# Seven quarter products in place of eight for the second matrix product of a fused attention and channel-mixer kernel

## The chip, the cores and the metric

The kernel runs on one core of a Trainium2 chip. The metric is the device time of one execution in microseconds (us). A core has a matrix engine (TensorE, PE in the profile, with its weight loads as PEld), two engines for elementwise work (VectorE, DVE; ScalarE, ACT), GpSimd (POOL), and queues that issue transfers (SP for most small ones, GpSimd for the large loads). Matrix products are written into PSUM banks of 128 partitions by 512 fp32 numbers; VectorE or ScalarE has to read a bank out before it can be used again.

## The reference

Selective attention over 8 batches, 8 heads, 576 positions, head size 64, then a low-rank sequence mixer and a channel mixer. What the change touches is the last line but one:

```
x = attention(q, k, v, s)            # per batch 576 x 512
h = (x^T @ U) @ V                    # rank 32, along the sequence
u = x + h^T                          # 576 x 512 per batch
ch = max(u @ w_ch1, 0) @ w_ch2       # 512 -> 2048 -> 512
return u + ch
```

`w_ch1` is 512 x 2048 and `w_ch2` 2048 x 512. The kernel takes and gives fp32 and multiplies in bf16.

## The kernel before

Heads are worked on in pairs: n = 0 to 31, four pairs to a batch. For each pair there are three generators, each of which yields after a piece of work:

- `transposes(n)` turns q and k with TensorE into two `pwork` banks; VectorE (for some n ScalarE) copies them into a `slot` (L309, L312). SP adds four bias rows to the slot from a table in HBM (L273).
- `scores(n)` multiplies q and k into `pscore` banks and a small `pwork` tail (L376), ScalarE takes the exponential into `pT` (L391, L402, L408), and VectorE masks (L321).
- `values(n)` multiplies pT with v into two `pwork` banks (L436); VectorE takes a reciprocal (L445) and scales into `x_sb` (L446).

`seqmix(b)` is the low-rank mixer of a batch: `up` (L465), a copy `uxT` on VectorE (L474), a product with the identity (L478), a copy `ux` on VectorE (L480), a product into one `pscore` pair and two `pwork` banks (L510), and their evacuation with an add on VectorE into `uT` (L490), with a small product for the last 64 rows (L535).

`chanmix(g)` is the channel mixer of 512 rows; there are nine groups (0 to 8), and group g needs rows of the batches g-1 and g. It has 16 steps of the first product: hidden tile nf is four matmuls of 128 x 512 into one `pwork` bank (L622), which ScalarE rectifies into `hT` as bf16 (L654). Then come four row tiles i of the second product, each 16 matmuls of 512 columns into one bank (L632); VectorE adds `u_sd`, a copy of uT turned back by a DMA transpose (L692), and SP writes the rows out (L709). The last row tile of group 8 is split into 384 and 128 columns (L669, L676, L682). Group 0 adds u by matmuls instead (L700, L708).

`pwork` has four banks that are given out in turn, `pscore` two double banks. Everything above that goes through `pwork`, the hidden tiles included, takes the next of its four.

The steps of `chanmix` are woven between the steps of attention as filling: `step_fill()` adds `pace[1]` to a counter after each attention step and lets one filling step run when the counter reaches 16. In the main loop (n = 8 to 33) the pace is 11 at first and 13 from the second batch on. What is left of the groups when attention ends runs alone with pace 16. In the steady part a batch takes about 38.5 us; from about 300 us on only groups remain.

The order of TensorE and of GpSimd is the order in which the program is written. For VectorE, ScalarE and SP that holds in the first part of the kernel; after that the scheduler of the tile framework puts their instructions into a fixed order when the kernel is built. All engines then execute their own order strictly one after another; each instruction waits on semaphores for what it needs.

Loads: GpSimd issues q, k and v of batch b+1 at the start of batch b (`load`, L111 and L182); v has three slots in rotation (`v_slots`), `slot` five, `uT` four, `u_sd` two.

Of the kernel before, what the change touches and what calls it, by code (L numbers as in the profile page):

```python
# [16 lines left out]
ALU = mybir.AluOpType  # L17
# [22 lines left out]
def kernel(  # L40
# [130 lines left out]
    def init_v(eng, vt):  # L171
        eng.memset(vt[64:, 4, :, :], 0.0)
        eng.memset(vt[:, 0:4, :, D : D + 1], 1.0)
        eng.memset(vt[0:64, 4, :, D : D + 1], 1.0)

    def load_v(b, parts=range(5)):
        vt = v_slots[b % 3]
        if b < 3:
            init_v(nc.gpsimd, vt)
        for t in parts:  # L180
            rows_t = 128 if t < 4 else 64
            nc.gpsimd.dma_start(  # L182
                out=vt[:rows_t, t, :, 0:D],
                in_=v[b, :, ds(t * 128, rows_t), :].rearrange("h p d -> p h d"),
            )
# [10 lines left out]

    SK = 5 * 128
    slots = [consts.tile([128, 2, S + SK], BF16, name=f"slot{i}") for i in range(NSLOT)]
    for slot in slots:
        nc.vector.memset(slot[:KA, :, 2 * S :], 0.0)  # L200

# [24 lines left out]
    for r, n_r, c in ((0, 3, 1), (3, 1, 0)):  # L226
# [4 lines left out]

    w1_sb = consts.tile([128, 4, FF], BF16)
    w2_sb = consts.tile([128, NF, DM], BF16)
    nc.gpsimd.dma_start(
        out=U_sb[:, :4, 0:R], in_=moe_U[:512].rearrange("(kt kp) r -> kp kt r", kp=128)
    )
# [18 lines left out]

    def uT(g):
        if g not in uT_of:
            uT_of[g] = work.tile([128, 4, 512], BF16, tag="uT", name="uT", bufs=4)
        return uT_of[g]


# [5 lines left out]

    def transposes(n):
        b, hp = divmod(n, PB)
        slot = slots[n % NSLOT]  # L270
        if b > 0:
            for r, n_r, c in ((0, 3, 1), (3, 1, 0)):
                nc.sync.dma_start(  # L273
                    out=slot[ds(D + r, n_r), :, ds(c * S, S)],
                    in_=rows_hbm[ds(r, n_r), ds(2 * n, 2)],
                )
        tps = {}

        def turn(hh, c):
            if c == 0:  # L280
                tile = pwork()
                if (n, hh) == (3, 0):
                    spin(2, tile)
                tps[hh] = tile.bitcast(BF16)[:, : 2 * 4 * TP].rearrange(
                    "p (c t m) -> p c t m", c=2, t=4
                )
            src = (q_t[b], k_t[b])[c]
            for t2 in range(4):
                nc.tensor.transpose(  # L289
                    tps[hh][:, c, t2, :],  # L290
                    src[:, 2 * hp + hh, ds(t2 * 128, 128)],
                    identity[:TP, :TP],
                )

        if b == 0:
            for hh in range(2):
                turn(hh, 0)
            yield
        for hh in range(2):
            if b > 0:  # L300
                turn(hh, 0)
            turn(hh, 1)
            tp = tps[hh]
            dst = slot[0:D, hh, 0 : 2 * S]
            for par in range(2):
                src = tp[par * D : par * D + D]
                if in_runs(b):
                    by_run = dst.rearrange("p (c t two m) -> p c t two m", c=2, t=4, two=2)
                    copies(n, hh, par)(by_run[:, :, :, par, :], src)  # L309
                else:  # L310
                    in_turn = dst.rearrange("p (c m t two) -> p c m t two", c=2, t=4, two=2)
                    copies(n, hh, par)(  # L312
                        in_turn[:, :, :, :, par], src.rearrange("p c t m -> p c m t")
                    )
            yield
# [54 lines left out]
        yield  # L370

    def scores(n, pT, spins=()):
        slot = slots[n % NSLOT]

        def mm(dst, hh, j, lo, hi):
            nc.tensor.matmul(  # L376
                dst,
                lhsT=slot[0:KA, hh, ds(S + j * 128, 128)],
                rhs=slot[0:KA, hh, lo:hi],
                start=True,  # L380
                stop=True,
            )

        tail = None
        for hh in range(2) if n > 0 else ():
            near = pscore()
            for j in range(4):
                mm(near[:, ds(j * 128, 128)], hh, j, j * 128, j * 128 + 128)
            mm(near[:, 512:960], hh, 0, 128, S)
            mm(near[:, 960:1024], hh, 3, 512, S)  # L390
            nc.scalar.activation(pT[:, hh, 0:1024], near, EXP, scale=scale)  # L391
            if n >= PB:
                mask(pT[:, hh, 0:512].rearrange("p (a b) -> p a b", a=4), 4, 128)
            if spins:
                tail = tail or pwork()
                spin(spins[hh], tail)
            yield
        mid, tail = pscore(), tail or pwork()
        for hh in range(2):
            mm(mid[:, ds(hh * 512, 320)], hh, 1, 256, S)  # L400
            mm(mid[:, ds(hh * 512 + 320, 192)], hh, 2, 384, S)
        nc.scalar.activation(  # L402
            pT[:, :, 1024:1536], mid.rearrange("p (a b) -> p a b", a=2), EXP, scale=scale
        )
        yield
        for hh in range(2):
            mm(tail[:, ds(hh * 64, 64)], hh, 4, 512, S)
        nc.scalar.activation(  # L408
            pT[:, :, 1536:1600],
            tail[:, 0:128].rearrange("p (a b) -> p a b", a=2),  # L410
            EXP,
            scale=scale,
        )
        if n >= PB:
            mask(pT[:, :, 1536:1600], 2, 64)
        yield
# [7 lines left out]
    def values(n, pT):  # L424
        b, hp = divmod(n, PB)
        if hp == 0:
            x_of[b] = work.tile([128, PB, 5, 128], BF16, tag="x_sb", name="x_sb")
            if b >= FT:
                xT_of[b] = work.tile([128, 4, 640], BF16, tag="xT", name="xT", bufs=1)
        x_sb, vt = x_of[b], v_slots[b % 3]  # L430
        for hh in range(2):
            h = 2 * hp + hh
            po = pwork()[:, : 5 * (D + 1)].rearrange("p (i d) -> p i d", i=5)
# [196 lines left out]
    def outputs(f2, hT, i, nfs, more=True):  # L630
        for nf in nfs:
# [8 lines left out]
            if nf % 4 == 3 and nf < nfs[-1]:  # L640
                yield

    def chanmix(g, hT=None, done=0):
        u = uT_of.pop(g)
        if g > 0:
            hT = work.tile([128, NF, 512], BF16, tag="hT", name="hT")
            u_sd = work.tile([128, 4, 4, 128], BF16, tag="u_sd", name="u_sd")
            nc.sync.dma_start_transpose(
                out=u_sd.rearrange("p a b c -> p (a b) c"), in_=u.rearrange("p a b -> p (a b)")
            )  # L650
        for nf in range(done, NF):
            f1 = pwork()
            hidden(f1, u, nf, range(4))
            nc.scalar.activation(hT[:, nf, :], f1, RELU)  # L654
            yield
        ahead = {}
        if g == 0:
            for i in range(2):
# [2 lines left out]
                    yield  # L661
                yield
        for i in range(4):
            if g == NG - 1 and i == 3:
                o_sb = work.tile([128, DM], FP32, tag="o_sb", name="o_sb", bufs=3)
                for lo, hi in ((0, 3), (3, 4)):
                    f2 = pwork()
                    for nf in range(NF):
                        nc.tensor.matmul(  # L669
                            f2[:, lo * 128 : hi * 128],  # L670
                            lhsT=hT[:, nf, ds(i * 128, 128)],
                            rhs=w2_sb[:, nf, lo * 128 : hi * 128],
                            start=(nf == 0),
                            stop=(nf == NF - 1),
                        )
                    nc.vector.tensor_tensor(  # L676
                        o_sb[:, lo * 128 : hi * 128].rearrange("p (a b) -> p a b", b=128),
                        f2[:, lo * 128 : hi * 128].rearrange("p (a b) -> p a b", b=128),
                        u_sd[:, lo:hi, i, :],
                        op=ALU.add,  # L680
                    )
                    nc.sync.dma_start(  # L682
                        out=out_flat[ds(g * 512 + i * 128, 128), lo * 128 : hi * 128],
                        in_=o_sb[:, lo * 128 : hi * 128],
                    )
                return
            f2 = ahead[i] if i in ahead else pwork()
            for _ in outputs(f2, hT, i, range(8 if i in ahead else 0, NF), g == 0):
                yield
            o_sb = work.tile([128, DM], FP32, tag="o_sb", name="o_sb", bufs=3)  # L690
            if g > 0:
                nc.vector.tensor_tensor(  # L692
                    o_sb.rearrange("p (a b) -> p a b", a=4),
                    f2.rearrange("p (a b) -> p a b", a=4),
                    u_sd[:, :, i, :],
                    op=ALU.add,
                )
            else:
                for dt in range(4):
                    nc.tensor.matmul(  # L700
                        f2[:, ds(dt * 128, 128)],
# [128 lines left out]
    def load(b):  # L830
        alloc_qk(b)
        for h in range(0, H, 4 if b == 2 else H):
            load_qk(b, h, 4 if b == 2 else H)
        load_v(b)

    load(2)
    fill.append(chanmix(0, first_hT, 4))
    pace[1] = 0
    made = {}
# [33 lines left out]
    for n in range(2 * PB, NP + 2):  # L873
# [20 lines left out]
            fill_with(1)  # L894
        if hp == 1 and b > FT:
            fill.append(chanmix(b - 1))
            pace[1] = 13
        if 2 * PB < n <= NP:
            run(values(n - 1, pT_of(n - 1)))
    pace[1] = 16  # L900
    fill.append(chanmix(NG - 1))
    while fill:
# [32 lines left out]
```

The softmax here doesn't subtract the row's maximum and nothing guards it: scores larger than these inputs give would overflow.

## Time and profile before

| | us |
|---|---|
| median of 9 executions | 375.37 |
| lowest and highest | 374.77, 381.16 |
| the profiled execution | 374.77 |
| its span, first to last instruction | 373.0 |
| TensorE busy | 364.5 |
| ScalarE busy | 199.1 |
| VectorE busy | 189.9 |
| GpSimd busy | 83.3 |

All parts of the profile come from this one execution. The span leaves out 1.8 us that lie around the first and last instruction. Matmuls are pipelined, so a matmul's own duration (379 ns for 512 columns) is longer than the distance to the next one; the latter is what counts for a row of them. TensorE is busy 9 tenths or more of nearly every fortieth of the span, and its clock is granted in full. In a row of instruction groups the columns are: line, engine, operation, output <- inputs, shapes, count, then busy time and mean duration of one, then idle time of the engine just before them and what ended it. Line numbers are those of the kernel before.

### The profile page before, as it was taken

How to read it: one execution, taken by the hardware profiler on the slowest of the kernel's cores; microseconds unless marked ns; L12 is line 12 of the kernel's file. 1: busy time of each engine (PE TensorE's matmuls, PEld its weight loads, DVE VectorE, ACT ScalarE, POOL GpSimd, SP SyncE). 2: the span in 40 equal slices, each digit the busy share in tenths (PEclk: the TensorE clock that was granted, in tenths of full speed). 3: DMA queues.
4: the chain of work that ended last, by engine and by line, in shares of the span. 5: the costliest groups of instructions: out<-in, count | busy, mean ns of one | idle time of the engine just before them, and what ended most of it. 6: DMA issues, size and time to landing. Idle time of an engine off the chain costs nothing.

```text
span 373.0 us, 8446 instructions
## 1 busy us (share of the span) xinstructions
PE 364.5 (98%) x3524; PEld 211.4 (57%) x3583; DVE 189.9 (51%) x446; ACT 199.1 (53%) x301; POOL 83.3 (22%) x108
## 2 busy tenths in 40 slices
PE   8999999999999999999999999999999999999996
PEld 4675566666655565556656565666565544444443
DVE  8876777585567545755475437653653142002011
ACT  3876965757742776067804782378435611621710
POOL 8997437115103600251006100000000000000000
PEclk9999999999999999999999999999999999999999
DMA  7999999999997993699969994210323043302002
GB/s 106 171 204 203 174 186 114 162 153 94 120 79 133 132 112 57 138 104 110 65 125 109 133 74 90 86 53 18 58 76 92 19 39 125 64 30 84 0 30 84
DMA packets 143534, 37.34 MB, mean 100 GB/s; under 512 B 130632, under 2 KB 137896, under 8 KB 143496
## 3 DMA queue, kind: packets, MB, share of 16 engines
q0 software_dynamic: 104640, 18.49, 84.9%
q1 hardware_dynamic: 38856, 18.31, 27.4%
q8 instruction: 28, 0.46, 0.6%
q14 instruction: 10, 0.08, 0.1%
HBM read 37.25 MB, written 9.70 MB: 126 GB/s over the span
## 4 chain that ended last, share of the span: by engine, by line
PE 92%; DVE 3%; ACT 2%; issue 2%; ACTq 0%
PE pwork L632 32%; PE pwork L622 31%; PE pscore L376 10%; PE pwork L436 7%; PE pwork L289 4%; PE pscore L338 1%; DVE slot L312 1%; PE pscore L205 1%; PE pwork L669 1%; PE pscore L622 1%; PE pwork L465 1%; DVE x_sb L446 1%; ACT pT L402 1%; PE pscore L510 1%; ACT pT L391 0%
## 5 line engine op out<-in xcount | busy, mean ns | idle before, releaser
L622 PE MATMUL pwork<-uT,w_sb 128*128 128x512 bf16 x533 | 134.0, 379 | 1.7 <-ACT pT L408 0.2
L632 PE MATMUL pwork<-w_sb,hT 128*128 128x512 bf16 x531 | 129.9, 379 | 1.8 <-DVE slot L312 0.2
L654 ACT ACTIVATE hT<-pwork 128x512 bf16<-128x512 f32 x140 | 84.8, 609 | 74.1 <-PE pwork L622 74.0
L391 ACT ACTIVATE pT<-pscore 128x1024 bf16<-128x1024 f32 x56 | 56.2, 1029 | 60.8 <-PE pscore L376 60.7
L622 PEld LDWEIGHTS <-w_sb 128*128 128x128 bf16 x576 | 50.8, 98 | 49.6 <-issue 0.6
L632 PEld LDWEIGHTS <-hT 128*128 128x128 bf16 x560 | 49.2, 98 | 49.0 <-issue 1.7
L321 DVE TENSOR_TENSOR pT<-pT,keep 128x512 bf16<-128x512 bf16 (+1 forms) x81 | 28.8, 355 | 59.8 <-ACT pT L391 36.0
L376 PE MATMUL pscore<-slot 68*128 68x320 bf16 (+1 forms) x500 | 54.6, 246 | 0.2
L376 PEld LDWEIGHTS <-slot 68*128 68x128 bf16 x564 | 41.6, 97 | 22.9 <-issue 1.3
L692 DVE TENSOR_TENSOR o_sb<-pwork,u_sd 128x512 f32<-128x512 f32 x31 | 21.4, 690 | 58.3 <-PE pwork L632 57.7
L436 PEld LDWEIGHTS <-pT 128*128 128x128 bf16 x870 | 33.1, 98 | 11.0 <-issue 0.3
L182 POOL DMA_DIRECT2D v_slot<-in_v_dram x36 | 30.3, 852 | 29.8 <-issue 17.7
L436 PE MATMUL pwork<-v_slot,pT 128*128 128x65 bf16 x870 | 35.3, 193 | 0.0
L309 DVE COPY slot<-pwork 64x576 bf16<-64x576 bf16 x70 | 31.7, 453 | 5.3 <-PE pwork L289 4.7
L446 DVE TENSOR_TENSOR x_sb<-pwork,rec 128x320 bf16<-128x320 f32 x64 | 31.5, 492 | 2.2
L402 ACT ACTIVATE pT<-pscore 128x1024 bf16<-128x1024 f32 x29 | 30.3, 1044 | 1.9 <-PE pscore L376 1.0
L312 DVE COPY slot<-pwork 64x576 bf16<-64x576 bf16 x35 | 28.1, 802 | 5.9 <-PE pwork L289 4.0
L111 POOL DMA_DIRECT2D q_sd<-in_q_dram x5 | 11.2, 2235 | 86.2 <-PE pwork L289 84.3
L445 DVE RECIPROCAL rec<-pwork 128x5 f32<-128x5 f32 x64 | 12.3, 192 | 24.4 <-PE pwork L436 24.0
L289 PEld LDWEIGHTS <-q_sd 72*128 72x128 bf16 x256 | 14.6, 98 | 9.7 <-DMA q_sd<-in_q_dram 0.9
L289 PE MATMUL pwork<-identity,q_sd 72*128 72x72 bf16 x256 | 18.4, 197 | 0.1
L289 PE MATMUL pwork<-identity,k_sd 72*128 72x72 bf16 x256 | 18.0, 197 | 0.0
(110 smaller groups left out, 223.3 us busy)
## 6 DMA issues: line engine op xcount, KB each, us to landing
out_dram<-o_sb SPq DMA_DIRECT2D x35, 256.0 KB
w_sb<-in_moe_w_ch_dram POOLq DMA_DIRECT2D x4, 1024.0 KB, 12.8
v_slot<-in_v_dram POOLq DMA_DIRECT2D x28, 128.0 KB, 16.2
q_sd<-in_q_dram POOLq DMA_DIRECT2D x5, 576.0 KB, 11.6
k_sd<-in_k_dram POOLq DMA_DIRECT2D x5, 576.0 KB, 17.8
q_sd<-in_q_dram POOLq DMA_DIRECT2D x4, 288.0 KB, 15.4
k_sd<-in_k_dram POOLq DMA_DIRECT2D x4, 288.0 KB, 14.1
q_sd<-in_q_dram POOLq DMA_DIRECT2D x4, 144.0 KB, 4.3
```

Source lines behind the costliest of these rows:

```text
L182: nc.gpsimd.dma_start(out=vt[:rows_t, t, :, 0:D], in_=v[b, :, ds(t * 128, rows_t), :].rearrange("h p d -> p h d"),)
L289: nc.tensor.transpose(tps[hh][:, c, t2, :], src[:, 2 * hp + hh, ds(t2 * 128, 128)], identity[:TP, :TP],)
L309: copies(n, hh, par)(by_run[:, :, :, par, :], src)
L312: copies(n, hh, par)(in_turn[:, :, :, :, par], src.rearrange("p c t m -> p c m t"))
L376: nc.tensor.matmul(dst, lhsT=slot[0:KA, hh, ds(S + j * 128, 128)], rhs=slot[0:KA, hh, lo:hi], start=True, stop=True,)
L391: nc.scalar.activation(pT[:, hh, 0:1024], near, EXP, scale=scale)
L402: nc.scalar.activation(pT[:, :, 1024:1536], mid.rearrange("p (a b) -> p a b", a=2), EXP, scale=scale)
L436: nc.tensor.matmul(po[:, i, :], lhsT=pT[:, hh, ds(place(j, i), 128)], rhs=vt[:, j, h, :], start=(j == 0), stop=(j == i), skip_group_check= ...
L446: nc.vector.tensor_tensor(x_sb[:, hp, :, ds(hh * D, D)], po[:, :, 0:D], rec.to_broadcast([128, 5, D]), op=ALU.mult,)
L622: nc.tensor.matmul(f1, lhsT=w1_sb[:, kt, ds(nf * 128, 128)], rhs=u[:, kt, :], start=(kt == 0), stop=(kt == 3),)
L632: nc.tensor.matmul(f2, lhsT=hT[:, nf, ds(i * 128, 128)], rhs=w2_sb[:, nf, :], start=(nf == 0), stop=(nf == NF - 1 and not more), skip_grou ...
L654: nc.scalar.activation(hT[:, nf, :], f1, RELU)
```

## The change

For groups 1 to 8 the second product is cut into quarters. With the hidden matrix A (512 rows by 2048) and w2 (2048 by 512),

```
A = [A11 A12]   rows 0-255        B = [B11 B12]   hidden 0-1023
    [A21 A22]   rows 256-511          [B21 B22]   hidden 1024-2047
```

the plain way has eight products of quarters. The change forms sums and makes seven, a form of Strassen's scheme:

```
A_1 = A21 + A22   A_2 = A_1 - A11   A_3 = A11 - A21   A_4 = A12 - A_2
B_1 = B12 - B11   B_2 = B22 - B_1   B_3 = B22 - B12   B_4 = B21 - B_2
p1 = A11 B11   p2 = A12 B21   p3 = A_4 B22   p4 = A22 B_4
p5 = A_1 B_1   p6 = A_2 B_2   p7 = A_3 B_3
C11 = p1 + p2             U2 = p1 + p6
C12 = U2 + p5 + p3        C21 = U2 + p7 + p4       C22 = U2 + p7 + p5
```

(The code subtracts B_4 the other way round from the classical scheme, so that all results are sums.) Each product is 2 x 8 matmuls of 256 columns into one `pwork` bank. The sums of w2 are formed once by GpSimd (12 instructions after the load of batch 2, and four at the start of group 1, which overwrite B12). The sums of A are formed by VectorE in halves of 128 x 1024 bf16; two of the eight are issued after hidden tiles 12 and 14, the others during p1, p2 and p6. A_1, A_2 and A_4 lie in two slots and one v slot that are no longer used otherwise; A_3 overwrites A21 in `hT`. The sums of the products with u are eleven VectorE instructions of 128 x 512 in fp32 and one copy of p1 on ScalarE. Outputs are written by quarters of 256 rows by 256 columns.

To make room, `slot` uses three of its five tiles from n = 8 on, v two of its three slots from batch 3 on (so `load_v` moves to the end of an iteration), `uT` has three buffers, `u_sd` one, and u_sd's transpose is issued at hidden tile 3. A group has 30 filling steps instead of 32, and the pace of the main loop becomes 12.

```diff
+    def weight_sums():
+        for dst, a, b in ((B_1, B12, B11), (B_2, B22, B_1), (B_4, B21, B_2)):
+            for k2 in range(0, HF, 2):
+                at = (slice(None), slice(k2, k2 + 2))
+                nc.gpsimd.tensor_sub(dst[at], a[at], b[at])
...
+    def total(dst, a, b, op, k4):
+        at = (slice(None), slice(4 * k4, 4 * k4 + 4))
+        nc.vector.tensor_tensor(dst[at], a[at], b[at], op=op)
+
+    def first_sums(hT, one):
+        if one:
+            total(A_1, hT[:, :HF, 256:], hT[:, HF:, 256:], ALU.add, 0)
+        else:
+            total(A_2, A_1, hT[:, :HF, :256], ALU.subtract, 0)
...
+        def product(acc, a, b, i):
+            for kt in range(HF):
+                nc.tensor.matmul(
+                    acc[:, i, :],
+                    lhsT=a[:, kt, ds(i * 128, 128)],
+                    rhs=b[:, kt, :],
+                    start=(i == 0 and kt == 0),
+                    stop=(kt == HF - 1),
+                    skip_group_check=True,
+                )
...
+        p1 = bank()
+        for i in halves:
+            product(p1, A11, B11, i)
+            total(*((A_1, A21, A22, ALU.add), (A_2, A_1, A11, ALU.subtract))[i], 1)
+            yield
+        nc.scalar.copy(U2, p1)
+        p2 = bank()
+        for i in halves:
+            product(p2, A12, B21, i)
+            total(A_3, A11, A21, ALU.subtract, i)
+            yield
+        o = quarter()
+        add_u(o, U2, 0, 0)
+        add(o, o, p2)
+        send(o, 0, 0)
+        p6 = bank()
+        for i in halves:
+            product(p6, A_2, B_2, i)
+            total(A_4, A12, A_2, ALU.subtract, i)
+            yield
+        add(U2, U2, p6)
+        p5 = bank()
...
+        add(o22, U2, p5)
+        p3 = bank()
...
+                add_u(o12, o22, 0, 1)
...
+        add(o12, o12, p3)
+        send(o12, 0, 1)
+        p7 = bank()
...
+                add_u(o22, o22, 1, 1)
...
+        add(U2, U2, p7)
+        add(o22, o22, p7)
+        send(o22, 1, 1)
+        p4 = bank()
...
+                add_u(o21, U2, 1, 0)
...
+        add(o21, o21, p4)
+        send(o21, 1, 0)
...
+            if g > 0 and nf in (12, 14):
+                first_sums(hT, nf == 12)
...
-        load_v(b)
 
     load(2)
+    load_v(2)
+    weight_sums()
...
-            pace[1] = 13
+            pace[1] = 12
...
+        if hp == 0 and 2 <= b < B - 1:
+            load_v(b + 1)
```

## The prediction

> **What bounds the kernel now.** I read the busy shares first, then the busy time by stretch, then the chain of waits, then the rows of the operations concerned, last the end of the timeline.
>
> The engines over the whole span:
>
> ```profile
> PE 364.5 (98%) x3524; PEld 211.4 (57%) x3583; DVE 189.9 (51%) x446; ACT 199.1 (53%) x301; POOL 83.3 (22%) x108
> ```
>
> TensorE (PE) is the only full engine. The same by stretch (columns: length, then busy time of PE, weight loads, VectorE, ScalarE, GpSimd; one batch of the steady part, the last stretch, in which the mixer runs alone):
>
> ```profile
> 148.64:187.09 38.45, 38.07 (x399) 22.64 (x407) 21.19 (x54) 22.16 (x35) 8.68 (x7) 1.00 1.67 107
> ...
> 330.00:373.00 43.00, 39.97 (x198) 18.97 (x200) 5.69 (x9) 9.55 (x16) 0.00 (x0) 1.00 0.14 50
> ```
>
> VectorE (DVE) has 17.3 us free in a batch of 38.45 us, and nearly everything in the last stretch. The chain of waits in order of time (start, length, what):
>
> ```profile
> 86.65 1.04 PE pwork L436 x30
> ...
> 342.51 9.28 PE pwork L622 x43
> ...
> 366.68 3.51 PE pwork L669 x32
> ```
>
> The chain is TensorE's own order. From it come the paces: 9.28/43 = 0.2158 us for a matmul of 512 columns; 16 of 384 with 16 of 128 take 3.51 us; the 30 of 65 columns, each with its own weight load, take at most 1.04 us, under 0.035 us each. So columns set the pace and weight loads hide, down to 65 columns. The rows I price VectorE and ScalarE with (busy, mean ns, idle before):
>
> ```profile
> L321 DVE TENSOR_TENSOR pT<-pT,keep 128x512 bf16<-128x512 bf16 x54 | 22.8, 422 | 36.2 <-ACT pT L391 36.0
> L692 DVE TENSOR_TENSOR o_sb<-pwork,u_sd 128x512 f32<-128x512 f32 x31 | 21.4, 690 | 58.3 <-PE pwork L632 57.7
> L321 DVE TENSOR_TENSOR pT<-pT,keep 128x128 bf16<-128x128 bf16 x27 | 6.0, 223 | 23.6 <-ACT pT L408 23.6
> L593 ACT CAST uT<-pwork 128x512 bf16<-128x512 f32 x4 | 2.3, 585 | 4.7 <-PE pwork L585 3.6 <-PE pwork L577 1.1
> ```
>
> Two facts of the timeline matter: VectorE's evacuation of the sequence mixer, and the end.
>
> ```profile
> 148.85 1.28 DVE L490 TENSOR_TENSOR uT<-pscore,xT 128x640 bf16<-128x640 f32 x2
> 150.05 1.41 DVE L490 TENSOR_TENSOR uT<-pwork,xT 128x320 bf16<-128x320 f32 x4
> ...
> 369.32 0.56 DVE L676 TENSOR_TENSOR o_sb<-pwork,u_sd 128x384 f32<-128x384 f32 x1 [1.91 <-PE pwork L669]
> 369.91 0.96 SPq L682 DMA_DIRECT2D out_dram<-o_sb  x2
> 370.21 0.29 DVE L676 TENSOR_TENSOR o_sb<-pwork,u_sd 128x128 f32<-128x128 f32 x1 [0.34 <-PE pwork L669]
> ```
>
> **What the Trainium skill says.** "TensorE: Matmul & The Clock Gate" (section "Wait — 56ns, not 53.3ns?") gives start to start N/2.4 GHz + 2.5 ns; for 512 columns 215.8 ns, which is what the trace has. "VectorE: DVE Perf Modes" ("The perf-mode tier table") gives tensor_tensor two elements a cycle for bf16 in SBUF and one for fp32 or PSUM; the rows agree, 223 and 422 ns at 128 and 512 bf16, 690 ns at 512 fp32. "SBUF — State Buffer" ("Who interferes with whom") says that a VectorE instruction with two SBUF inputs and a GpSimd one that reads SBUF exclude each other; this trace has no GpSimd arithmetic on two inputs, so it is not shown here.
>
> **The change part by part.**
>
> *Fewer columns.* A group's second product now takes 64 x 0.2158 = 13.8 us (the last group 48 x 0.2158 + 3.49 = 13.85). Afterwards it is 7 x 2 x 8 = 112 matmuls of 256 columns at 256/2400 + 0.0025 = 0.1092 us, 12.2 us. Saved 1.58 us a group, 12.7 us over eight. All of it lies on the path. Were the 256-column pace 0.125 us, nothing would be left; the 65-column row speaks against that.
>
> *Pace of the weaving.* A group yields 30 times instead of 32, and the pace goes from 13 to 12 sixteenths: 0.906 and 0.9 groups a batch. Nothing moves between stretches; cost 0.
>
> *More on VectorE.* A group had 4 adds, 2.8 us. It gets 8 sums of 1024 bf16 elements and 11 adds of 512. From 223 and 422 ns a bf16 sum costs 0.157 us + 0.000518 us per element, 0.69 us at 1024; the sums are 5.5 us, the adds 11 x 0.69 = 7.6 us, together 13.1 us. ScalarE's copy of the first product, 0.585 us, lies in its free time (22 of 38 us busy) and costs 0.
>
> All this falls into one part of the group, from hidden tile 13 to the last product. I counted in the changed kernel's own order per engine what else lies there (mean durations of before; PE by columns): groups 1 to 6 need VectorE for 26.4, 25.2, 25.7, 26.4, 24.7, 17.2 us, PE for 22.4, 22.1, 22.1, 22.1, 21.5, 16.5 us. The surpluses are 4.0, 3.1, 3.6, 4.3, 3.2, 0.7, sum 18.9 us. Groups 7 and 8 run alone: 13.1 against 14.8 us, no surplus.
>
> Does the surplus reach PE? PE runs ahead only as far as the four pwork banks allow. I followed group 3 by hand, t=0 at the end of its hidden tile 15. VectorE does uxT to 0.9, two slot copies 1.9, sum 2.6, mask 3.0, two sums 4.4, mask 4.8, ux 5.1. PE reaches the product with ux (L510) at 4.7, so it waits 0.5 us. It reaches p6, the third product, at 6.9; the rotation gives p6 the bank that p2 held, which VectorE's add of p2 sets free; that add stands behind another (5.8), a sum (6.5), a mask (6.7) and four evacuations of the sequence mixer (8.6) and ends at 9.2: 2.4 us more. Nothing later in the group waits. Together 2.9 us. Likewise group 1: 2.3 us for banks of values tiles and of p2, 0.3 for ux, 1.9 for p5's bank, 4.5; group 2: ux 1.0, p6's bank 1.8, p3's 0.3, 3.1; group 4: uxT behind four sums 1.4, ux 0.2, then two banks behind evacuations that stand behind a sum of hidden tile 15, 3.1, 4.7. These four give 15.2 us, their surpluses 15.0, so I use the surplus for groups 5 and 6: 19.1 us. I used durations; back to back VectorE starts sooner (1.41 us for four operations whose durations add to 1.65). Some 0.7 us a group come off: 15 us taken. Bounds: 5 us, if the hidden tiles' lighter part (8.5 to 9.4 us of VectorE in 17 us) absorbs the lag; 24 us, if VectorE also idles in its fixed order.
>
> *GpSimd sums.* Twelve subtractions of 512 elements stand between the loads of batch 2 and batch 3, four more in group 1. "GPSIMD Engine Reference" ("Elementwise — side-by-side cycle accounting") has 2.6 cycles an element at 1.2 GHz: my estimate is 1.1 us and 0.15 us of dispatch, so 12 take 15 us. Batch 3's q was issued at 56.1 us, so now near 69; q and k take 4.5 us to issue and, at median, 11.6 and 17.8 us to land: k at 91 us. Its first transpose ran at 88.4. Six masks fall beside the subtractions and can each be held 1.2 us. Between 0 and 6 us; I take 1.5. The four in group 1 delay batch 4's load by 5 us of 36 spare.
>
> *Moved loads and buffers.* load_v goes to the end of an iteration and needs two slots; V of batch b+1 is used a batch later (38 us) and lands in 16 us, so 0. Three slots instead of five: a slot was last read an iteration (9 us) before it is written; 0. One u_sd, three uT: u_sd's transpose is issued at hidden tile 3, some 5 us after the group before ended, and used 12 tiles later; 0. On SP's queue its transpose and the outputs wait for VectorE ahead of the next slot's bias rows; these are wanted about 9 us later, which covers a lag of 2 to 3 us, and beyond that each us counts once.
>
> *The end.* Now PE ends at 370.2, the last add 0.3 us later, a 64 KB output lands 2.4 us after issue. Afterwards three 0.69 us operations follow p7 while p4 runs 1.75 us, then the last add: PE's end + 1.1 us. The last output is 256 KB: +0.7 us (0 to 1.5; the trace has no landing for it). Together +1.5 us.
>
> Sum: -12.7 + 15 + 1.5 + 1.5 = +5.3 us on the profiled execution's own 374.77 us (span 373.0), 380.1. The median of the runs shown is 0.6 us above it; 380.5.
>
> **The rivals.**
>
> *A, VectorE's queue takes over in the woven part* (as above): 376 to 388. For it: surpluses counted, one in-order queue feeding four banks. Against it: VectorE averages only 86% of a batch (19.3 + 0.9 x 13.1 = 31.1 us of 36.3).
>
> *B, the lag is absorbed*: stalls of 3 to 8 us, no stall from GpSimd: 374.8 - 12.7 + 1.5 + 5 = 368.6. This is the faster one. It decides if banks are on average free within about 1.5 us a group: below 10 us of stalls in all the kernel wins. For it: PE waits nowhere in the steady part now, and start to start VectorE is quicker than its durations.
>
> *C, GpSimd's subtractions hold VectorE's masks and batch 3's k*, on top of A: 6 us in place of 1.5 and the 24 us bound: 374.8 - 12.7 + 24 + 1.5 + 6 = 393.6.
>
> *D, no shorter product*: weight loads or the start cost of 256-column matmuls eat the gain; then A's stalls stay, near 393. The 65-column pace makes this unlikely.
>
> **How the numbers follow.** A 0.57, B 0.32, C 0.08, D 0.03. The range 367 to 391 holds B and A and leaves out C's and D's end and B's best. A's own is 376 to 388. The measurement tells 0.2% (0.75 us) from no change. Faster: B and the low edge of A, 0.34; same 0.05; slower the rest, 0.61.
>
> **What would show it.** Products at 0.109 us each in TensorE's rows; sums at 0.69 us; VectorE near full in each group's second half, with TensorE idle there, waiting for "DVE o_sb", "DVE uT" or "DVE ux", 2 to 5 us a group, none in groups 7 and 8; a last chain item of VectorE. It is wrong if PE stays at 98% (B), if products run above 0.12 us (D), or if PE's idle time sits before 95 us (C).

## The result, and the profile after

| | before | after |
|---|---|---|
| median, us | 375.99 (53 executions) | 380.97 (16 executions) |
| lowest and highest | 374.73, 384.80 | 377.37, 383.16 |
| the profiled execution | 374.77 | 378.01 |
| its span | 373.0 | 376.2 |

The ratio of after to before is 1.0109, with a 95% interval of 1.0085 to 1.0133: the change makes the kernel 1.1% slower. The number is within 0.5 us of the forecast of 380.5. The profile shows that most of the reasons behind it are not those of the forecast. In some executions TensorE runs at a lower clock for a stretch and the kernel takes longer; the ratios leave the longest of those out, the medians don't, and where the two tell different things this is the reason.

Line numbers are now those of the kernel after: the hidden tiles are L643 (L653 in group 0), the quarter products L688, scores L397, values L457, masks L342, the scaling into `x_sb` L466 and L467, the sequence mixer's evacuation L511, the sums of A L670, the adds L702, the sums of w2 L254 and L785.

The page (busy time over the span, then fortieths of it: TensorE's busy share and its granted clock, both in tenths):

```profile
PE 355.1 (94%) x3907; PEld 249.2 (66%) x3951; DVE 270.1 (72%) x565; ACT 204.5 (54%) x309; POOL 101.3 (27%) x124
...
PE   8999993699999999999999999999999999999995
...
PEclk9999998699999999999999999999999999999999
```

TensorE has fallen from 98% to 94% of the span, and not evenly: the hole lies in the seventh and eighth fortieth, from 56 to 75 us, where the granted clock drops as well. That is long before the first quarter product of the kernel (112.79 us in the timeline). VectorE works 80 us more than before (11.7 of them are one held instruction, shown below), and apart from this hole only the first and the last fortieth of TensorE fall below 9 tenths. TensorE's waits (what waited, for what, total us, times, longest):

```profile
PE pwork L397 <- DVE x_sb L467: 9.5, 1, 9.5
...
PE pwork L688 <- DVE o_sb L702: 0.7, 2, 0.4
```

One single wait of 9.5 us, and next to nothing from the adds that the forecast feared. The timeline around it:

```profile
55.02 4.49 POOL L254 TENSOR_TENSOR w_sum<-w_sb 128x512 bf16<-128x512 bf16 x4
...
56.58 0.49 DVE L467 TENSOR_TENSOR x_sb<-pwork,rec 128x320 bf16<-128x320 f32 x1
...
56.99 11.66 DVE L342 TENSOR_TENSOR pT<-pT,keep 128x512 bf16<-128x512 bf16 x1
...
59.48 8.89 POOL L254 TENSOR_TENSOR w_sum<-w_sb,w_sum 128x512 bf16<-128x512 bf16 x8
...
68.57 0.18 DVE L466 RECIPROCAL rec<-pwork 128x5 f32<-128x5 f32 x1
...
69.34 0.29 PE L397 MATMUL pwork<-slot 68*128 68x64 bf16 x2 [9.51 <-DVE x_sb L467]
...
69.85 1.49 PE L653 MATMUL pwork<-w_sb,hT 128*128 128x512 bf16 x3 [0.22 <-issue]
```

A mask (the third row), which takes 0.42 us elsewhere, begins at 56.99 us and ends at 68.65, 0.3 us after the last of GpSimd's twelve subtractions (59.48 + 8.89 = 68.37). VectorE is held here to the end of GpSimd's whole row of instructions, not of one of them. The reciprocal and the scaling that wait behind this mask are the ones that free the `pwork` banks, so TensorE is out of banks for 9.5 us. When it starts again, three matmuls of 512 columns take 1.49 us; at 75.44 us three such take 0.81. The same stretches in windows (length; busy time of PE, weight loads, VectorE, ScalarE, GpSimd; clock; DMA share; GB/s):

```profile
54.40:69.34 14.94, 5.38 (x73) 3.63 (x73) 14.24 (x11) 3.00 (x3) 14.92 (x14) 0.79 1.47 54
...
69.34:72.00 2.66, 2.44 (x17) 1.56 (x19) 1.20 (x5) 0.28 (x1) 2.66 (x2) 0.50 0.24 15
72.00:76.00 4.00, 3.94 (x55) 2.81 (x54) 2.78 (x6) 2.18 (x3) 0.79 (x1) 0.85 1.92 115
76.00:80.00 4.00, 4.00 (x57) 2.79 (x56) 2.63 (x7) 2.91 (x4) 2.78 (x4) 1.00 1.96 166
...
117.53:154.76 37.23, 36.69 (x443) 26.56 (x446) 28.02 (x68) 21.99 (x35) 8.70 (x8) 1.00 1.28 111
```

The second to fourth rows are the restart: TensorE is busy, first at half its clock, then (0.85 over 4 us) at half for another 1.2 us, then at full. "TensorE: Matmul & The Clock Gate" of the Trainium skill (section "Part 1: The HAM clock gate (the "warmup" mystery)") states half the clock until the array has been busy for about 3.4 us; the trace has 2.66 + 1.2 = 3.9 us. Half the clock for 3.9 us costs 1.9 us. The last row is a batch with quarter products in it, full of work and at full clock.

Where the time is won and lost can be read off landmarks in the two timelines, mostly the first matmul of the sequence mixer of each batch (L465 before, L486 after):

| landmark | before | after | difference |
|---|---|---|---|
| first hidden tile of group 0 (L622, L643) | 28.70 | 29.64 | +0.9 |
| the two score matmuls behind the 9.5 us wait | 58.70 | 69.34 | +10.6 |
| sequence mixer of the second batch | 68.94 | 81.27 | +12.3 |
| third | 104.82 | 117.53 | +12.7 |
| fourth | 142.49 | 154.76 | +12.3 |
| fifth | 180.94 | 191.81 | +10.9 |
| sixth | 219.40 | 229.14 | +9.7 |
| seventh | 257.86 | 266.45 | +8.6 |
| eighth | 298.07 | 305.34 | +7.3 |
| end of TensorE | 370.2 | 372.0 | +1.8 |
| end of the span | 373.0 | 376.2 | +3.2 |

All of the loss is there at 81 us: 0.9 us from the start on, 9.7 us in the hold, 1.7 us in the restart. The 0.9 us are not the change's: of the kernels below, the one of before with subtractions added has its first hidden tile at 29.66 us, and one with all the quarter products (e9) at 28.83. From then on the kernel is faster in nearly every batch and wins back 10.5 us, of the 12.7 us that the columns were to save. The chain of waits holds the mask, and the quarter products of the last group (start, length, what):

```profile
57.07 11.58 DVE pT L342
...
359.80 10.49 PE pwork L688 x96
```

The matmuls of the products run at 10.49/96 = 0.1093 us each, the forecast's 0.1092. The rows of the operations that the forecast priced (busy, mean ns, idle before):

```profile
L670 DVE TENSOR_TENSOR slot<-slot,hT 128x1024 bf16<-128x1024 bf16 x16 | 11.0, 689 | 0.3
L702 DVE TENSOR_TENSOR o_sb<-o_sb,u_sd 128x512 f32<-128x512 f32 x16 | 11.0, 688 | 0.3
...
L254 POOL TENSOR_TENSOR w_sum<-w_sb,w_sum 128x512 bf16<-128x512 bf16 x8 | 8.9, 1138 | 0.0
```

The first two prices were right (0.69 us each), the third 10% high: 1.25 us against 1.14, and in the row one begins 1.11 us after the other, so the 0.15 us of dispatch in the estimate doesn't show. What was wrong is what waits for what, and how long.

### The profile page after: what moved, and what is told of

It is laid out like the page before. It is cut to its first block, busy times and chain, and to the rows that moved or that the text cites. A ratio compares the mean times of both kernels' runs of the same rounds, so it can differ in the third digit from the quotient of the medians.

```text
span 376.2 us, 9369 instructions
## 1 busy us (share of the span) xinstructions
PE 355.1 (94%) x3907; PEld 249.2 (66%) x3951; DVE 270.1 (72%) x565; ACT 204.5 (54%) x309; POOL 101.3 (27%) x124
## 4 chain that ended last, share of the span: by engine, by line
PE 76%; DVE 13%; ACT 5%; issue 3%; DMA 2%; SPq 0%; DVEq 0%; ACTq 0%
PE pwork L643 29%; PE pwork L688 21%; PE pscore L397 9%; PE pwork L457 7%; DVE pT L342 3%; PE pwork L310 3%; PE pwork L653 3%; ACT hT L789 2%; DVE uT L511 2%; DVE o_sb L702 2%; DVE slot L670 2%; ACT pT L412 1%; DMA slot<-hT 1%; PE pscore L643 1%; DVE slot L333 1%
## 5 line engine op out<-in xcount | busy, mean ns | idle before, releaser
L643 PE MATMUL pwork<-uT,w_sb 128*128 128x512 bf16 x525 | 133.6, 379 | 2.4 <-ACT hT L789 0.5
L643 PEld LDWEIGHTS <-w_sb 128*128 128x128 bf16 x576 | 50.7, 98 | 50.0 <-issue 0.9
L397 PEld LDWEIGHTS <-slot 68*128 68x128 bf16 x564 | 41.3, 97 | 26.6 <-DVE x_sb L467 9.6
L342 DVE TENSOR_TENSOR pT<-pT,keep 128x512 bf16<-128x512 bf16 (+1 forms) x81 | 40.9, 505 | 22.7 <-ACT pT L412 15.7
L397 PE MATMUL pscore<-slot 68*128 68x320 bf16 (+1 forms) x500 | 56.0, 246 | 0.3 <-DMA slot<-hT 0.2
L688 PEld LDWEIGHTS <-hT 128*128 128x128 bf16 x512 | 47.7, 98 | 7.7 <-issue 0.7
L688 PE MATMUL pwork<-w_sb,hT 128*128 128x256 bf16 x384 | 47.5, 273 | 0.0
L457 PEld LDWEIGHTS <-pT 128*128 128x128 bf16 x870 | 32.4, 98 | 5.3 <-issue 0.6
L457 PE MATMUL pwork<-v_slot,pT 128*128 128x65 bf16 x870 | 35.5, 193 | 0.2 <-DVE uT L511 0.2
L688 PE MATMUL pwork<-w_sum,slot 128*128 128x256 bf16 x256 | 31.5, 272 | 0.8 <-DVE o_sb L702 0.7
L467 DVE TENSOR_TENSOR x_sb<-pwork,rec 128x320 bf16<-128x320 f32 x64 | 31.2, 488 | 1.4
L670 DVE TENSOR_TENSOR slot<-hT 128x1024 bf16<-128x1024 bf16 x16 | 11.0, 687 | 24.5 <-ACT hT L789 24.3
L688 PEld LDWEIGHTS <-slot 128*128 128x128 bf16 x256 | 24.1, 98 | 4.5 <-issue 1.6
L466 DVE RECIPROCAL rec<-pwork 128x5 f32<-128x5 f32 x64 | 12.1, 190 | 20.7 <-PE pwork L457 20.3
L702 DVE TENSOR_TENSOR o_sb<-o_sb,pwork 128x512 f32<-128x512 f32 x32 | 21.8, 681 | 1.0 <-PE pwork L688 0.3
## 6 DMA issues: line engine op xcount, KB each, us to landing
q_sd<-in_q_dram POOLq DMA_DIRECT2D x5, 576.0 KB, 12.6
```

The lines of the kernel that those rows point to most:

```text
L342: nc.vector.tensor_tensor(dst, dst, keep[:, :, 0:w].to_broadcast([128, n_tiles, w]), op=ALU.min)
L397: nc.tensor.matmul(dst, lhsT=slot[0:KA, hh, ds(S + j * 128, 128)], rhs=slot[0:KA, hh, lo:hi], start=True, stop=True,)
L457: nc.tensor.matmul(po[:, i, :], lhsT=pT[:, hh, ds(place(j, i), 128)], rhs=vt[:, j, h, :], start=(j == 0), stop=(j == i), skip_group_check= ...
L467: nc.vector.tensor_tensor(x_sb[:, hp, :, ds(hh * D, D)], po[:, :, 0:D], rec.to_broadcast([128, 5, D]), op=ALU.mult,)
L643: nc.tensor.matmul(f1, lhsT=w1_sb[:, kt, ds(nf * 128, 128)], rhs=u[:, kt, :], start=(kt == 0), stop=(kt == 3),)
L688: nc.tensor.matmul(acc[:, i, :], lhsT=a[:, kt, ds(i * 128, 128)], rhs=b[:, kt, :], start=(i == 0 and kt == 0), stop=(kt == HF - 1), skip_g ...
```

## The experiments

Two theories were to be told apart. L: GpSimd's subtractions hold VectorE for as long as they run, and this is the whole loss. Q: VectorE's queue in the woven groups costs about 15 us, as the forecast had it, and the hold in the trace is a coincidence. All kernels start from the kernel after unless said otherwise, and the edits are shown in part. The kernel before has medians of 375.70 to 375.73 us beside them; ratios are to the kernel before, with a 95% interval.

**No sums of w2.** The sixteen subtractions are left out and the products take plain quarters, as many and as large; what they compute is not the reference.

```diff
-    B_1, B_2, B_4 = (consts.tile([128, HF, HD], BF16, name=f"w2_sum{i}") for i in (1, 2, 4))
-    B_3 = B12
+    B_1, B_2, B_3, B_4 = B11, B22, B12, B21
...
-    weight_sums()
```

> The changed kernel without the sixteen GpSimd subtractions: the quarters of w2 are used as they are, so B_1 to B_4 are left out of what is computed; everything else stands. Theory L (the run of subtractions on GpSimd keeps one VectorE mask from starting until the run is over, and TensorE stands behind that mask): the time falls by 12 us or more against the changed kernel, to about 366 us (375.4 - 12.7 of columns + 1.4 at the end + 2 of stalls in the woven part), ratio to before about 0.975, and no mask above 1 us. Theory Q (the predicted one: VectorE's longer queue costs TensorE some 15 us in the second halves of the groups): the time falls by no more than 2 us, to about 379 us.

Measured: 366.42 us (365.65 to 366.92), ratio 0.9757 [0.9740, 0.9774]. The fourth batch in windows:

```profile
143.42:180.48 37.06, 37.06 (x447) 26.81 (x445) 28.94 (x69) 22.37 (x34) 8.80 (x8) 1.00 1.46 110
```

TensorE has no gap in it, with VectorE busy for 28.94 of 37.06 us. So the subtractions cost 380.97 - 366.42 = 14.5 us, and everything else in the change together makes the kernel 9.3 us faster. This is L, not Q.

**The kernel before with the twelve subtractions** in the same place, into a tile that nobody reads.

```diff
+    spare = consts.tile([128, 8, 256], BF16, name="spare")
+    def weight_sums():
...
+                nc.gpsimd.tensor_sub(spare[at], a[at], b[at])
...
     load(2)
+    weight_sums()
```

> The kernel before with twelve GpSimd subtractions of the same size at the same place (after the load of batch 2), into a tile that nobody reads. L: one mask near 57 us lasts about 11 us and the time rises by 10 to 14 us, to 386 to 389 us. Q: they run in GpSimd's free time; 375 to 377 us.

Measured: 390.25 us (386.89 to 391.21), ratio 1.0377 [1.0329, 1.0426]: 14.5 us slower than before, with no other edit, and just above the 386 to 389 us that L had. Its timeline:

```profile
54.22 13.33 POOL L258 TENSOR_TENSOR spare<-w_sb 128x512 bf16<-128x512 bf16 x12
54.25 13.37 DVE L329 TENSOR_TENSOR hT<-hT,keep 128x128 bf16<-128x128 bf16 x1
...
68.44 1.00 PE L444 MATMUL pwork<-v_slot,pT 128*128 128x65 bf16 x15 [12.56 <-DVE x_sb L454]
```

Here it is the small mask, 0.2 us elsewhere, that lasts 13.37 us. Nothing of the change but the subtractions is needed for the loss, and it is the same 14.5 us whether the twelve are added to one kernel or all sixteen taken from the other. The wait also is longer than in the trace of after, 12.56 us against 9.51, since here the mask before the one of 56.99 us is caught. In after that mask ran at 54.23 us, 0.8 us ahead of the first subtraction. After's own sixteen times lie in two heaps, four from 377.37 to 378.09 us, the profiled one among them, and eleven from 380.01 to 383.16, with one between; that the slower ones are those in which the earlier mask is caught fits the 3 us between them, but no trace of such an execution was taken. In the profiled one the hold and the restart cost 9.7 + 1.7 = 11.4 us, so the 14.5 us of the medians are those of the heap with the longer times.

**A gap after each subtraction**: a short GpSimd instruction that only writes, to see whether VectorE gets in between.

```diff
...
                 nc.gpsimd.tensor_sub(dst[at], a[at], b[at])
+                nc.gpsimd.memset(gap, 0.0)
```

> The changed kernel with a small GpSimd memset (256 elements, writes only) after each of the twelve subtractions. L with a port that is given away between two reading instructions: the mask lasts 1 to 2 us, TensorE's stall goes, about 367 us. L with a hold that lasts as long as GpSimd has work: the run gets longer (12 x 0.3 us), the mask lasts about 15 us, about 382 to 385 us. Q: 380 to 381 us, as the changed kernel.

Measured: 383.43 us (382.15 to 384.39), ratio 1.0200 [1.0173, 1.0227]; TensorE's wait is now 14.9 us. The timeline:

```profile
54.95 15.72 DVE L345 TENSOR_TENSOR hT<-hT,keep 128x128 bf16<-128x128 bf16 x1
...
55.57 0.32 POOL L257 MEMSET gap<- 128x256 bf16 x1
...
55.84 1.15 POOL L256 TENSOR_TENSOR w_sum<-w_sb 128x512 bf16<-128x512 bf16 x1
...
69.44 1.14 POOL L256 TENSOR_TENSOR w_sum<-w_sb,w_sum 128x512 bf16<-128x512 bf16 x1
...
70.53 0.30 POOL L257 MEMSET gap<- 128x256 bf16 x1
```

The mask is held through all twelve subtractions and the memsets between them, and ends at 70.67 us: 0.1 us after the last subtraction (69.44 + 1.14 = 70.58) and within the record of the last memset. So a memset between two subtractions doesn't let VectorE in, though it leaves 0.2 us from the end of one to the start of the next (the first subtraction ends at 55.64 us, the second begins at 55.84, within the memset's record); and VectorE got in before GpSimd had stopped, after the last instruction that reads.

**The sums of w2 on VectorE**, one behind each hidden tile of group 1.

```diff
-                nc.gpsimd.tensor_sub(dst[at], a[at], b[at])
+                yield nc.vector.tensor_sub(dst[at], a[at], b[at])
...
             nc.scalar.activation(hT[:, nf, :], f1, RELU)
+            if g == 1:
+                next(sums, None)
```

> The changed kernel with all sixteen sums of w2 on VectorE, one after each hidden tile of group 1, none on GpSimd. L: about 366 us, 9 us faster than before; 16 x 0.42 us of VectorE lie in a stretch with room. Q: VectorE's queue gets 6.7 us longer, so not below 380 us.

Measured: 376.99 us (374.57 to 382.40), ratio 1.0010 [0.9987, 1.0033]. A miss, and for a reason of place:

```profile
49.08 0.81 DVE L333 COPY slot<-pwork 64x576 bf16<-64x576 bf16 x1
55.97 0.43 DVE L254 TENSOR_TENSOR w_sum<-w_sb,w_sum 128x512 bf16<-128x512 bf16 x1 [6.08 <-DMA w_sb<-in_moe_w_ch_dram]
```

The scheduler that orders VectorE moved twelve of the sums (those of B_1, B_2 and B_4) from group 1 to 44 to 63 us, where their only input, w2, was still being loaded; the four of B_3 stayed, at 88 to 92 us. In the profiled execution, which took 381.68 us, VectorE stood 6.1 us for the load with slot copies behind it, and TensorE 5.9 us for those. An instruction with early inputs need not stay where the program has it.

**The same, bound to its place**: `behind` makes the instruction just written depend on the one of the given engine that precedes it in the program; on VectorE itself this fixes the order and needs no semaphore.

```diff
...
+                nc.vector.tensor_sub(dst[at], a[at], b[at])
+                behind(tc, E.DVE, mybir.DependencyClass.NoSync)
+                yield
...
```

> As the run before with the sums of w2 on VectorE, but each sum is bound behind the VectorE instruction that the program has ahead of it, so that none is pulled forward to where w2 has not landed. L (only the hold by GpSimd and, in the last run, the early place cost time): 366 to 368 us, ratio 0.975 to 0.98, no wait of VectorE for the load of w2. If VectorE's queue is what costs: 372 us or more.

Measured: median 370.29 us of six (366.17 to 375.73), ratio 0.9783 [0.9713, 0.9852]. The median is above the expected 366 to 368. In the profiled execution, of 372.30 us, TensorE's clock was granted at 0.64 to 0.67 from 10 to 30 us, before any part of the change; in the two shortest, 366.17 and 366.22 us, its mean was 0.998 and 1.0. These two are at e1's time with the sums made, and so is the last version below, which makes the same sums: five of its six took 365.64 to 366.71 us. Sixteen sums of 0.41 us each, spread over the woven stage, cost nothing that can be seen.

**The sums on GpSimd, but single**: each waits for a step of TensorE, and q and k of batch 3 are issued ahead of them.

```diff
...
                 nc.gpsimd.tensor_sub(dst[at], a[at], b[at])
+                behind(tc, E.PE, mybir.DependencyClass.Sync)
+                yield
...
```

> The sixteen sums of w2 stay on GpSimd, but one at a time: each waits for the TensorE step it is put behind, some 2 us apart, so that GpSimd is idle between two of them; batch 3's q and k are issued ahead of them. L with a hold that ends when GpSimd runs out of work: masks of at most 1.6 us, no stall of TensorE above 1 us, 366 to 369 us. L with a hold that comes from the number of subtractions wherever they lie: still above 375 us.

Measured: 375.19 us (368.86 to 383.56), ratio 0.9886 [0.9849, 0.9923]: faster than before, but short of the sums on VectorE, and above the 366 to 369 that L had for it. The timeline of the profiled execution, which took 381.36 us, has several cases:

```profile
63.14 5.69 DVE L356 TENSOR_TENSOR pT<-pT,keep 128x512 bf16<-128x512 bf16 x1
...
64.06 4.47 POOL L266 TENSOR_TENSOR w_sum<-w_sb 128x512 bf16<-128x512 bf16 x4
68.50 1.33 POOL L266 TENSOR_TENSOR w_sum<-w_sb,w_sum 128x512 bf16<-128x512 bf16 x1
...
76.82 1.15 POOL L266 TENSOR_TENSOR w_sum<-w_sb,w_sum 128x512 bf16<-128x512 bf16 x1 [0.62 <-PE pwork L667]
76.90 1.35 DVE L356 TENSOR_TENSOR pT<-pT,keep 128x512 bf16<-128x512 bf16 x1 [0.64 <-ACT pT L426]
...
78.39 3.45 POOL L266 TENSOR_TENSOR w_sum<-w_sb,w_sum 128x512 bf16<-128x512 bf16 x3 [0.41 <-PE pwork L667]
...
80.07 0.74 DVE L356 TENSOR_TENSOR pT<-pT,keep 128x128 bf16<-128x128 bf16 x1
```

GpSimd reached its first sums late, found their TensorE steps done, and ran four in a row: that mask was held through the four and ended at 68.83 us, 0.3 us after them (64.06 + 4.47 = 68.53), though the fifth sum had begun at 68.50; the fifth lasted 1.33 us, 0.2 us more than the others. Where a sum stood alone, the mask lasted 1.35 us, to that sum's end (77.97) and 0.3 us on. In the row of three (78.39 to 81.84) the small mask was held for 0.74 us and ended at 80.81, with the row still running. TensorE waited 3.7 and 3.2 us for VectorE.

So single subtractions hold VectorE less than a row, as L has it, but "as long as GpSimd has work" is too simple. In the kernel before with subtractions added no mask got in at any of the eleven changes from one subtraction to the next; here it did twice, with no gap between the two in the records. These sums each wait for a step of TensorE; whether that is what lets VectorE in, no run shows. The first mask's record begins 0.9 us ahead of the first subtraction; no run shows why.

**VectorE's own limit.** If the queue costs next to nothing, more of it should. In the kernel without sums of w2, every sum of A is made a second time, into a tile that nobody reads (sixteen in place of eight a group); then half of them (twelve); then none at all, with plain quarters of A in the products. None of the three computes the reference.

```diff
+    twice = consts.tile([128, HF, HD], BF16, name="twice")
     def total(dst, a, b, op, k4):
         at = (slice(None), slice(4 * k4, 4 * k4 + 4))
+        nc.vector.tensor_tensor(twice[at], a[at], b[at], op=op)
         nc.vector.tensor_tensor(dst[at], a[at], b[at], op=op)
```

> The kernel without sums of w2 (its output leaves them out) and every sum of A made twice, the second copy into a tile that nobody reads: 8 more VectorE instructions of 0.69 us in each group. If VectorE's queue has room (the reading of the last runs: 28 to 29 us busy of 37 in a batch): at most 2 us above the kernel with single sums, 366.5 to 368.5. If the queue is near its edge: 0.5 us per instruction or more of the woven groups, 371 us and above.

> The kernel without the sums of w2, with four of the eight sums of A in each of groups 1 to 8 made a second time: twelve in place of eight, half of what the doubling added (384.8 us). The output leaves out the sums of w2. If the stall grows in proportion from eight sums on: 366.4 + 9 = 375 us, within 3. If there is an edge between twelve and sixteen sums: 366 to 369. The second would say that the change as written has at least four sums a group (2.8 us) of slack in VectorE's queue.

> All the sums ahead of the products are left out: neither the sixteen of w2 nor the eight of A in each of groups 1 to 8 (the products take plain quarters instead, so the output is not the reference's). Against the kernel without the sums of w2 alone (366.4 us) only VectorE's queue is relieved, by 8 x 0.69 = 5.5 us in each group. Lag absorbed (now held): 0 to 2 us lower, 364.5 to 366.4. VectorE's queue costs 15 us, as the prediction had it: 10 us or more lower, 352 to 357.

| sums of A in a group | median, us | against e1 | TensorE's main waits for VectorE |
|---|---|---|---|
| 0 (e9) | 364.41 (364.08 to 364.86) | -2.0 | none above 0.3, but for 1.3 at the start that every kernel has |
| 8 (e1) | 366.42 (365.65 to 366.92) | | o_sb 0.7 |
| 12 (e10) | 374.57 (373.69 to 381.69) | +8.2 | o_sb 3.4, uT 1.3, ux 0.8 |
| 16 (e7) | 384.82 (384.31 to 385.13) | +18.4 | ux 4.4, o_sb 4.1, uT 2.8, v_slot 1.1 |

The same batch of e9, e10 and e7 in windows, one fence each:

```profile
142.25:179.20 36.95, 36.68 (x443) 26.79 (x446) 25.38 (x62) 22.27 (x34) 8.68 (x8) 1.00 1.44 111
```

```profile
144.75:183.19 38.44, 37.37 (x443) 26.77 (x445) 31.03 (x73) 22.38 (x34) 8.80 (x8) 1.00 1.42 107
```

```profile
145.18:184.72 39.54, 37.24 (x447) 26.69 (x445) 32.46 (x76) 22.37 (x34) 8.79 (x8) 1.00 1.38 103
```

The eight sums of the change are 43.8 us of VectorE (64 x 0.685) and cost 2.0 us: nearly all absorbed. The next 32 are 21.9 us and cost 8.2; the 32 after these cost 10.3. So there is a bend, and it lies at about the change's own load, 29 us of VectorE in a batch of 37 (the order that the scheduler gives VectorE may differ among the four kernels; that was not looked at). For the doubled sums, the queue with room (366.5 to 368.5) was missed by far and the queue near its edge (371 and above) came true; for twelve, the stall that grows in proportion. The slack in VectorE's queue is about used up by the change as written. Q's mechanism is real, with the names that the forecast gave it (ux, uT, o_sb); it begins where the change ends.

**The best version.** On top of e5, the last product of group 8 goes into two banks, and each half is added and sent as it is ready.

```diff
...
+        if g == NG - 1:
+            o21 = quarter()
+            add_u(o21, U2, 1, 0)
+            for i in halves:
+                p4 = bank()
+                product(p4, A22, B_4, i, True)
...
+                send(o21, 1, 0, slice(i, i + 1))
+            return
```

> The late sums on VectorE, and the last product of group 8 in two banks, its first half added and sent while the second is multiplied. The last add falls from 0.69 to 0.42 us and the last output from 256 to 128 KB: 0.5 to 1 us below the kernel with late sums alone.

Measured: 366.35 us (365.64 to 374.15), ratio 0.9730 [0.9675, 0.9785]. The split gained nothing that can be seen against e5's two shortest executions, 366.2 us; 0.5 to 1 us was expected. From TensorE's last matmul to the end of the span it is 3.9 us here and 4.2 in e5, so 0.3 us were won there. The end in the timeline shows why not more:

```profile
358.68 1.91 PE L702 MATMUL pwork<-w_sum,hT 128*128 128x256 bf16 x16
358.88 0.69 DVE L716 TENSOR_TENSOR U<-U,pwork 128x512 f32<-128x512 f32 x1 [0.75 <-PE pwork L702]
359.49 0.68 DVE L716 TENSOR_TENSOR o_sb<-o_sb,pwork 128x512 f32<-128x512 f32 x1
360.08 0.68 DVE L716 TENSOR_TENSOR o_sb<-U,u_sd 128x512 f32<-128x512 f32 x1
360.87 0.76 DVE L716 TENSOR_TENSOR o_sb<-o_sb,pwork 128x256 f32<-128x256 f32 x2
```

The first half of the product is done before 360 us, but its add stands behind three others. VectorE's row of adds comes last, not the product, whatever the size of the last piece. Still, this version is 9.4 us faster than before and 14.6 us faster than the change as written.

## Why the forecast's number came out, and its reasons did not

The runs take the sum apart. The kernel before, 375.7 us, less the columns' 12.7 and with the end's 1.3, is 364.3; e9, which has neither sums of A nor of w2, took 364.41. Eight sums of A a group add 2.0 (e1 against e9), the hold adds 14.5 (after against e1, and, independently, e2 against before). Together 380.8, measured 380.97. So VectorE's queue cost 13 us less than forecast and the hold 13 us more. That the number came out is luck: two terms failed by the same amount, in opposite directions. (The forecast's own terms add up to 380.7, not 380.5.)

- *Fewer columns, -12.7*: right. 0.1093 us a matmul against 0.1092, and e9's total leaves 0.1 us unexplained. Rival D falls.
- *VectorE's queue, +15 (5 to 24)*: this term failed; it measured about 2 us (the sums of A; e9's total leaves 0.1 for the adds), below its lower bound. The failed step is the passing on: a surplus of VectorE's durations was taken to reach TensorE nearly in full, and it was nearly all absorbed. The walk through group 3 had TensorE wait 0.5 us for ux and 2.4 us at p6 for the bank of p2. The timeline of after has

```profile
196.27 0.29 DVE L501 CAST ux<-pwork 128x128 bf16<-128x128 f32 x1
...
196.74 0.39 PE L531 MATMUL pscore<-V_sb,ux 32*128 32x512 bf16 x2
...
197.95 1.91 PE L688 MATMUL pwork<-w_sum,slot 128*128 128x256 bf16 x16
...
199.67 0.67 DVE L702 TENSOR_TENSOR o_sb<-o_sb,pwork 128x512 f32<-128x512 f32 x1
...
200.40 1.03 PE L688 MATMUL pwork<-w_sum,slot 128*128 128x256 bf16 x8 [0.30 <-DVE o_sb L702]
...
213.58 0.92 DVE L330 COPY slot<-pwork 64x576 bf16<-64x576 bf16 x2 [0.20 <-PE pwork L310]
```

  The third row is p6. It starts 1.7 us before the add of p2 (fourth row) does, so it doesn't use that bank; p5 (the row after) waits for that add, and by then the wait is 0.30 us. The walk gave the banks out in another order than the kernel does, and p6, 1.9 us long, covers the lag. VectorE is some two microseconds behind here; the next hidden tiles begin at 211.13 us, and at 213.58 (last row) VectorE waits for TensorE again: the lag is gone, which is what rival B said.
- *GpSimd's subtractions, +1.5 (0 to 6)*: this term failed too; it measured 14.5 us. The step was "six masks ... can each be held 1.2 us": the hold was taken to last one GpSimd instruction. So does the Trainium skill have it: "SBUF — State Buffer" (section "SBUF: two separate sides") says of the two engines that whichever "starts first gets the pair for the whole instruction; the other fully blocks". The trace agrees on who is held: the scaling L467, with one input in SBUF, ran at 56.58 us beside the subtractions in 0.49 us, and the first mask after it didn't. It disagrees on how long: 11.66, 13.37 and 15.72 us, in these three to the end of the last of twelve subtractions. They should have been priced as one block of 13.3 us, in which VectorE stops at its first mask and TensorE soon after it, with the clock's restart on top. Batch 3's k, the other half of rival C, came in time: no wait for it is named after 60 us.
- *Moved loads, three slots, one u_sd*: cost 0, right; no wait names them.
- *The end, +1.5*: right, +1.3. From TensorE's last matmul to the end of the span it is 376.2 - 372.0 = 4.2 us against 2.9 before (370.18 to 373.04).

So the likeliest case, A, was wrong by the forecast's own sign (TensorE's idle time lies before 95 us, as it said for C), and what happened is B's absorbed lag with C's hold, at more than twice C's 6 us.

## What to carry to other kernels

A GpSimd subtraction of two inputs in SBUF is not background work as soon as VectorE has masks with two SBUF inputs: price a row of them as one block in which VectorE, and all that waits on it, stands still (13.4 us for twelve in e2), and put them where VectorE has none, or do them on VectorE (e5). A surplus of an engine over a stretch isn't a stall: follow which buffer each waiting instruction really gets, and measure the slack by adding work until the time moves. A forecast that hits can be two errors of opposite sign; read where the time is idle before believing it.

## What the runs showed of the hardware that was not expected

- A VectorE mask with two SBUF inputs, once caught behind GpSimd's subtractions, can be held through many of them: 13.37 us for twelve, 11.66 us for the same less the first and part of the second, 15.72 us with memsets between them, 5.69 us for four, 1.35 us where one stood alone. Each time it ended 0.1 to 0.3 us after the end of a subtraction. At which one VectorE gets in, and what decides it, isn't shown: in the rows of twelve it was the last, in e6 an earlier one. The twelve cost TensorE 9.5 us of bank waits in one kernel and 12.6 in another, depending on which mask was caught.
- After 9.5 us without work TensorE's clock was granted at 0.50 for some 3.9 us.
